# Wider moving operand in the second layer: one matmul of 512 columns in place of two of 256, tiles three to seven

## The chip, the cores and the metric

The kernel runs on one core of a Trainium2 chip. The metric is the device time of one execution in microseconds (us). A core has five engines that run side by side: TensorE (PE, matmuls; its weight loads are listed apart as PEld), VectorE (DVE), ScalarE (ACT), GpSimd (POOL) and SyncE (SP), which here issues the transfers (DMA).

## What is computed

Linear attention with positive random features (8 batches, 8 heads, 576 positions, 64 values per head, 128 features), followed by a layer norm and a two-layer perceptron with a residual. Cut to what matters:

```python
q_p, k_p = phi(q_s), phi(k_s)            # exp(projection - its maximum), 128 features
kv = np.einsum('bhsm,bhsd->bhmd', k_p, v)
z = np.sum(k_p, axis=2)
num = np.einsum('bhsm,bhmd->bhsd', q_p, kv)
den = np.einsum('bhsm,bhm->bhs', q_p, z)[..., None] + 1e-06
x = (num / den)                          # heads side by side: 4608 rows of 512
xn = (x - mu) / np.sqrt(var + 1e-06) * g_ln
ch = np.maximum(xn @ w_ch1, 0.0) @ w_ch2 # 512 -> 2048 -> 512
return x + ch
```

All of it is in 32-bit floats. The product that the change touches is the second one of the perceptron, hidden values (2048) by `w_ch2`.

## The kernel before, in words

**Tiling.** The 4608 rows are nine tiles of 512 rows (`NT`, `T`), each four chunks of 128 rows (`TC`). The 2048 hidden values are 16 blocks of 128 (`NF`). Weights and activations are each split into a rounded high part and a low rest, and a product is three matmuls: high by high, high by low, low by high.

**Three ways through the perceptron.** Tiles 0 and 1 (t < `SEVEN` = 2): the first layer is `mm1`, lines 1335 to 1355, and its matmuls go through the helper `rounded` (line 1299), 512 columns each. Tiles 2 to 6: the first layer is `seven` (line 1385), which computes two by two blocks with seven products instead of eight, each product six matmuls of 256 columns through `product` (line 1380). Tiles 7 and 8 (t >= `DEEP` = 7): both layers work that way, the second one in `deep` and `deep_product` (line 1659).

**The second layer, `mm2` (line 1606).** It serves tiles 0 to 6. One call handles one hidden block f of one tile t: for each of the four row chunks i it adds a 128x128 block of hidden values (stationary, `hl`) times a 128x512 block of weights (moving, `w`) to the bank `accs[i]` of PSUM, in three passes. In tiles 0 and 1 a pass is one matmul of 512 columns through `rounded`. In tiles 2 to 6 it is two matmuls of 256 columns at line 1627, one for each half of the output columns, each with its own weight load. So a call is 12 matmuls of 512 columns in the first two tiles and 24 of 256 columns in the next five. Columns are stored in an interleaved order, so each form reads its moving operand and writes PSUM in short strided pieces; both cover the same 512 output columns.

**The order of the work.** A planner (`Plan`) writes the order of all engines when the kernel is built: each generator says which engine it wants next and for how long, and the planner picks by rank and by its estimate of when each engine is free. `mm2` asks for `us(PE, 3 * 0.2268)` per row chunk (line 1619) whatever the tile. `gen_mlp` (line 1771) strings the perceptron together at the lowest rank: in tiles 2 to 6 `seven` runs four products, then lets one `mm2` call in (`between`), runs three more products, and another `mm2` call follows. Work of higher rank is put between: keys (`joined`, line 797; sums at line 747), queries (`gen_q2`, two matmuls of 512 columns through `rounded`, `om_hi` and `om_lo`) and the numerators of the attention (line 1104). Lines 747, 838, 885 and 1104 are small matmuls that use part of the array.

The evictions of a finished chunk (`result`, line 1638, on DVE) and the stores of the output come after the last block f of a tile.

Of the kernel before, what the change touches and what calls it, by code (L numbers as in the profile page):

```python
# [29 lines left out]
NF = DFF // P  # L30
# [38 lines left out]
class Plan:  # L69
# [74 lines left out]
    def free(self, *names):  # L144
        for n in names:
            assert n not in self.places, n
            self.places[n] = self.cur.seen()
            self.cur.holds -= n[0] == "b" and 0 < self.cur.holds
            self.wake(lambda w: w[0] == "get" and n in w[1])
# [48 lines left out]
def favor_ffn(ctx, tc, kT, kTr, kD, kDr, vF, vR, qT, qD, omT, gT, w1, w2, out):  # L198
# [12 lines left out]
    nc = tc.nc  # L211
# [24 lines left out]
    def us(eng, t):  # L236
        return "run", {eng: t}
# [16 lines left out]
    def wait(*key):  # L254
        return "wait", key
# [13 lines left out]
    def bank(tag, n=512):  # L269
        return tile_of(tag, [P, 512], F32, ps)[:, 0:n]  # L270
# [1026 lines left out]
    def rounded(out, lhsT, rhs, start, stop):  # L1297

        nc.tensor.matmul(  # L1299
            out.rearrange("p (c a b) -> p c a b", a=AW, b=BW), lhsT,  # L1300
            rhs.rearrange("p (a c b) -> p c a b", a=AW, b=BW), start=start, stop=stop,
        )
# [301 lines left out]
    accs = {}  # L1604

    def mm2(t, f):
        yield wait("w", 2, f)
        yield wait("hid", t, f)
        lent = f in LENT
        if lent and t >= SEVEN:  # L1610
            yield wait("back", t, f)
        t_h, hl = hid[t, f]
        w = wparts[2, f]
        for i in range(TC):
            if f == 0:
                t_b = yield "get", (b_acc[i],)
                accs[i] = bank(t_b)
            cs = slice(i * P, (i + 1) * P)
            yield us(PE, 3 * 0.2268)
            if t < SEVEN:  # L1620
                rounded(accs[i], hl[:, 0, cs], w[:, 0], start=(f == 0), stop=False)
                rounded(accs[i], hl[:, 0, cs], w[:, 1], start=False, stop=False)
                rounded(accs[i], hl[:, 1, cs], w[:, 0], start=False, stop=(f == NF - 1))
            else:
                for l, r in ((0, 0), (0, 1), (1, 0)):
                    for n in range(2):
                        nc.tensor.matmul(  # L1627
                            accs[i].rearrange("p (c a b) -> p c a b", a=AW, b=BW)[:, :, n * 8 : n * 8 + 8], hl[:, l, cs],
                            w[:, r, n * HC : (n + 1) * HC].rearrange("p (a c b) -> p c a b", b=BW, c=4),
                            start=f + l + r + n == 0, stop=f == NF - 1 and l == 1, skip_group_check=True,  # L1630
                        )
            if f == NF - 1:
                plan.add(URGENT + 50, result(t, i, accs[i]))
        free(t_h)
        if lent and t >= SEVEN - 1:
            free(*n_w[2, f + HOSTS if t >= SEVEN and f in SHARED else f])

    def result(t, i, acc):
        c = t * TC + i
        t_x, x = xs[c]  # L1640
        yield wait("rs", t)
        yield dve(DM)
        nc.vector.scalar_tensor_tensor(
            out=x, in0=acc, scalar=rss[:, c : c + 1], in1=x, op0=ALU.mult, op1=ALU.add
        )
        free(b_acc[i])
        yield dma(P * DM)
        nc.sync.dma_start(out[c * P : (c + 1) * P], x)
        free(t_x)
# [121 lines left out]
    def gen_mlp():  # L1771
# [8 lines left out]
        for t in range(NT):  # L1780
            for f in range(NF if t < SEVEN else NF // 2):
                if f == 0 and t < SEVEN:
                    yield from one()
                if t < SEVEN:
                    if t == f == 0:
                        yield from opening(OPEN)
                    elif t or f >= OPEN:
                        yield from mm1(t, f)
                    yield from one()
                    last.append(mm2(t, f))  # L1790
                else:
                    g, h = divmod(f, 2)
                    yield from seven(t, g, h, one)
                    yield from one()
                    if t < DEEP:
                        last += [mm2(t, NK * g + h), mm2(t, NK * g + 2 + h)]
                    else:
                        last += [deep(t, f, FRONTS), deep(t, f, BACKS)]
            if t >= DEEP:
                last.append(deep_late(t))  # L1800
# [47 lines left out]
AW, BW = 16, 8  # L1848
# [9 lines left out]
SEVEN, HC = 2, DM // 2  # L1858
# [72 lines left out]
```

## Time and profile before

| | |
|---|---|
| time, median of 3 runs | 926.13 us (925.30 to 926.68) |
| the profiled execution's own time | 925.38 us |
| its span, first to last instruction | 923.3 us |
| TensorE busy | 915.2 us (99%), 8893 matmuls and as many weight loads |
| VectorE busy | 794.7 us (86%) |
| ScalarE busy | 520.3 us (56%) |
| GpSimd busy | 139.0 us (15%) |
| line 1627, the matmuls in question | 1920, 239.1 us busy |
| granted TensorE clock, mean | 0.999 |

The profile's times are those of one execution. Matmuls are pipelined: a matmul starts while the one before is still in the array, so the duration that is listed for one is longer than the distance between two starts, and the busy time of a group is the union of its matmuls' spans. The timeline merges consecutive instructions of a kind into one row: its start, the time from its first start to its last end, and the count behind the x.

### The profile page before, as it was taken

Reading aid. Unit: us, or ns where it says so; the run is one execution under the profiler, and the core shown is the slowest. Engines: PE = TensorE matmul, PEld = TensorE weight load, DVE = VectorE, ACT = ScalarE, POOL = GpSimd, SP = SyncE. Lnnn points to the kernel's source line nnn. Section 1 sums busy time; section 2 is a strip of 40 time slices with the busy share of each in tenths; the row PEclk is TensorE's granted clock in tenths of the full one; section 3 lists DMA queues with packets and bytes.
Section 4 is the critical chain, followed back from the end, with each engine's and each line's share of the span. In section 5 each row is a group of like instructions: output and inputs, shape, how many; then the busy total and the mean of one; then the engine's idle time right before and its main releaser. Section 6 shows DMA issues by size and latency. Waiting matters only on the chain.

```text
span 923.3 us, 23130 instructions
## 1 busy us (share of the span) xinstructions
PE 915.2 (99%) x8893; PEld 855.1 (93%) x8893; DVE 794.7 (86%) x1810; ACT 520.3 (56%) x1227; POOL 139.0 (15%) x80
## 2 busy tenths in 40 slices
PE   9999999999999999999999999999999999999998
PEld 7787788888889999999999999999999999999997
DVE  7999998978987899879988899889888889778766
ACT  6687755545556467645754576456654544453442
POOL 3301423200221012201111032011201310000000
PEclk9999999999999999999999999999999999999999
DMA  9179852368897998898898998898777869999981
GB/s 346 71 260 381 276 179 94 92 184 239 262 306 263 333 332 282 282 346 272 284 322 269 314 336 281 283 343 292 269 233 239 271 195 301 379 327 298 362 285 46
DMA packets 150317, 247.62 MB, mean 268 GB/s; under 512 B 13120, under 2 KB 64448, under 8 KB 150208
## 3 DMA queue, kind: packets, MB, share of 16 engines
q1 hardware_dynamic: 150208, 246.16, 79.4%
q8 instruction: 70, 1.15, 0.5%
q14 instruction: 39, 0.32, 0.1%
HBM read 204.16 MB, written 41.94 MB: 267 GB/s over the span
## 4 chain that ended last, share of the span: by engine, by line
PE 95%; DVE 3%; DMA 1%; issue 0%; POOL 0%; ACT 0%; DVEq 0%; SPq 0%; ACTq 0%
PE b L1380 29%; PE b L1627 24%; PE b L1299 20%; PE b L1659 8%; PE b L747 4%; PE b L1104 4%; PE b L797 2%; PE b L838 2%; PE b L330 1%; PE b L885 1%; PE b L1326 1%; DMA wide<-qD 1%; DVE v L1703 0%; PE b L1284 0%; DVE kp L1748 0%; DVE x L1041 0%
## 5 line engine op out<-in xcount | busy, mean ns | idle before, releaser
L1627 PE MATMUL b<-w,hid 128*128 128x256 f32 x1920 | 239.1, 276 | 0.0
L1627 PEld LDWEIGHTS b<-w,hid 128*128 128x128 f32 x1920 | 229.0, 188 | 2.8
L950 POOL PARTITION_ALL_REDUCE wide<-wide x72 | 137.9, 1938 | 606.1 <-ACT wide L244 328.3
L1380 PE MATMUL b<-xnT,w 128*128 128x256 f32 x1344 | 174.5, 276 | 0.0
L1380 PEld LDWEIGHTS b<-xnT,w 128*128 128x128 f32 x1344 | 162.7, 188 | 1.6
L1380 PE MATMUL b<-w,w 128*128 128x256 f32 x1008 | 126.7, 276 | 0.2 <-DVE hid L1471 0.2
L1443 DVE TENSOR_TENSOR w<-b,w 128x256 f32<-128x256 f32 x224 | 108.5, 484 | 15.7 <-PE b L1380 9.9
L1380 PEld LDWEIGHTS b<-w,w 128*128 128x128 f32 x1008 | 120.2, 188 | 1.5 <-DVE hid L1471 0.4
L1299 PE MATMUL b<-w,hid 128*128 128x512 f32 x384 | 97.2, 392 | 0.0
L1299 PE MATMUL b<-xnT,w 128*128 128x512 f32 x360 | 89.8, 392 | 0.0
L1299 PEld LDWEIGHTS b<-w,hid 128*128 128x128 f32 x384 | 70.7, 188 | 14.9 <-issue 0.3
L1299 PEld LDWEIGHTS b<-xnT,w 128*128 128x128 f32 x360 | 66.5, 188 | 14.6 <-issue 1.0
L812 ACT ACTIVATE kp<-kp,mb 128x128 f32<-128x128 f32 x176 | 64.9, 398 | 18.9 <-DVE mb L809 18.8
L1469 ACT ACTIVATE hid<-w 128x256 fp32r<-128x256 f32 x82 | 42.7, 522 | 49.0 <-PE b L1627 27.8
L244 ACT COPY wide<-b 128x512 f32<-128x512 f32 x70 | 39.9, 584 | 38.8 <-PE b L1299 20.1
L958 ACT ACTIVATE wide<-wide 128x512 f32<-128x512 f32 x72 | 45.5, 633 | 26.9 <-DVE wide L953 26.6
L1471 DVE SCALAR_TENSOR_TENSOR hid<-w,hid 128x256 fp32r<-128x256 f32 x82 | 49.6, 606 | 12.5 <-ACT hid L1469 11.9
L953 DVE TENSOR_TENSOR wide<-wide,wide 128x512 f32<-128x512 f32 x64 | 49.3, 772 | 3.7 <-POOL wide L950 3.5
L1659 PE MATMUL b<-w,wide 128*128 128x256 f32 x348 | 45.3, 275 | 0.0
L914 DVE TENSOR_TENSOR wide<-wide,wide 64x512 fp32r<-64x512 f32 x56 | 41.6, 749 | 2.2 <-ACT wide L912 0.6
L1659 PEld LDWEIGHTS b<-w,wide 128*128 128x128 f32 x348 | 42.1, 188 | 0.0
L1469 ACT ACTIVATE hid<-b 128x256 fp32r<-128x256 f32 x40 | 15.3, 382 | 46.6 <-PE b L1380 41.9
(162 smaller groups left out, 1449.7 us busy)
## 6 DMA issues: line engine op xcount, KB each, us to landing
w<-side SPq DMA_DIRECT2D x224, 256.0 KB, 4.9
w<-kept SPq DMA_DIRECT2D x80, 512.0 KB, 4.7
w<-kept SPq DMA_DIRECT2D x67, 256.0 KB, 5.3
w<-w SPq DMA_DIRECT2D x32, 512.0 KB, 6.3
wide<-qD SPq DMA_DIRECT2D x56, 256.0 KB, 5.2
w<-deep SPq DMA_DIRECT2D x47, 256.0 KB, 5.4
wide<-kD SPq DMA_DIRECT2D x40, 256.0 KB, 5.2
kept<-w SPq DMA_DIRECT2D x16, 512.0 KB, 3.0
```

Source lines behind the costliest of these rows:

```text
L812: nc.scalar.activation(out=kp[:, j], in_=kp[:, j], func=AF.Exp, scale=1.0, bias=mb[:, j : j + 1])
L914: nc.vector.tensor_tensor(out=qs[D:P], in0=qraw[D:P], in1=f32(qs[D:P]), op=ALU.subtract)
L950: nc.gpsimd.partition_all_reduce(mx, qc, P, bass_isa.ReduceOp.max)
L953: nc.vector.tensor_tensor(out=qc, in0=pq if direct else qc, in1=mx, op=ALU.subtract)
L958: nc.scalar.activation(out=qc, in_=qc, func=AF.Exp)
L1299: nc.tensor.matmul(out.rearrange("p (c a b) -> p c a b", a=AW, b=BW), lhsT, rhs.rearrange("p (a c b) -> p c a b", a=AW, b=BW), start=start ...
L1380: nc.tensor.matmul(passes(out), left(k, l), passes(right[:, r, k]), start=start and k + l + r == 0, stop=k + r == 2, skip_group_check=True,)
L1443: nc.vector.tensor_tensor(out=out, in0=left, in1=right, op=ALU.add)
L1469: nc.scalar.activation(out=hl[:, 0, cols], in_=x, func=AF.Relu)
L1471: nc.vector.scalar_tensor_tensor(out=hl[:, 1, cols], in0=x, scalar=0.0, in1=f32(hl[:, 0, cols]), op0=ALU.max, op1=ALU.subtract)
L1627: nc.tensor.matmul(accs[i].rearrange("p (c a b) -> p c a b", a=AW, b=BW)[:, :, n * 8 : n * 8 + 8], hl[:, l, cs], w[:, r, n * HC : (n + 1) ...
L1659: nc.tensor.matmul(out.rearrange("p (c a b) -> p c a b", a=8, b=8), left[:, l, chunk * P : (chunk + 1) * P], right[:, r].rearrange("p (a c ...
```

## The change

The branch on t is removed from `mm2`: the three passes of tiles 2 to 6 go through `rounded`, 512 columns each, as in tiles 0 and 1. Nothing else is edited; the time that the planner is told stays as it was.

```diff
             cs = slice(i * P, (i + 1) * P)
             yield us(PE, 3 * 0.2268)
-            if t < SEVEN:
-                rounded(accs[i], hl[:, 0, cs], w[:, 0], start=(f == 0), stop=False)
-                rounded(accs[i], hl[:, 0, cs], w[:, 1], start=False, stop=False)
-                rounded(accs[i], hl[:, 1, cs], w[:, 0], start=False, stop=(f == NF - 1))
-            else:
-                for l, r in ((0, 0), (0, 1), (1, 0)):
-                    for n in range(2):
-                        nc.tensor.matmul(
-                            accs[i].rearrange("p (c a b) -> p c a b", a=AW, b=BW)[:, :, n * 8 : n * 8 + 8], hl[:, l, cs],
-                            w[:, r, n * HC : (n + 1) * HC].rearrange("p (a c b) -> p c a b", b=BW, c=4),
-                            start=f + l + r + n == 0, stop=f == NF - 1 and l == 1, skip_group_check=True,
-                        )
+            rounded(accs[i], hl[:, 0, cs], w[:, 0], start=(f == 0), stop=False)
+            rounded(accs[i], hl[:, 0, cs], w[:, 1], start=False, stop=False)
+            rounded(accs[i], hl[:, 1, cs], w[:, 0], start=False, stop=(f == NF - 1))
             if f == NF - 1:
                 plan.add(URGENT + 50, result(t, i, accs[i]))
```

## Rows read from the trace of the kernel before

**Rows 1.** The page: busy time of the engines, and the chain that ended last.
```profile
PE 915.2 (99%) x8893; PEld 855.1 (93%) x8893; DVE 794.7 (86%) x1810; ACT 520.3 (56%) x1227; POOL 139.0 (15%) x80
...
PE b L1380 29%; PE b L1627 24%; PE b L1299 20%; PE b L1659 8%; PE b L747 4%; PE b L1104 4%; PE b L797 2%; PE b L838 2%; PE b L330 1%; PE b L885 1%; PE b L1326 1%; DMA wide<-qD 1%; DVE v L1703 0%; PE b L1284 0%; DVE kp L1748 0%; DVE x L1041 0%
```

**Rows 2.** Windows: window and length, busy time (count) of each engine, clock, DMA.
```profile
275.90:770.50 494.60, 494.60 (x5292) 485.39 (x5291) 432.51 (x1008) 288.16 (x686) 79.24 (x43) 1.00 0.86 287
```

**Rows 3.** Groups by line and shape: busy us, mean ns, idle before.
```profile
L1627 PE MATMUL b<-w,hid 128*128 128x256 f32 x1920 | 239.1, 276 | 0.0
...
L1299 PE MATMUL b<-w,hid 128*128 128x512 f32 x384 | 97.2, 392 | 0.0
```

**Rows 4.** Timeline of PE, third tile: start us, length us, what.
```profile
275.99 2.88 PE L1627 MATMUL b<-w,hid 128*128 128x256 f32 x24
278.71 0.84 PE L1380 MATMUL b<-xnT,w 128*128 128x256 f32 x6
```

**Rows 5.** Timeline of PE, second tile, at 172 us.
```profile
172.52 2.80 PE L1299 MATMUL b<-w,hid 128*128 128x512 f32 x12
175.16 1.49 PE L1299 MATMUL b<-xnT,w 128*128 128x512 f32 x6
```

**Rows 6.** Timeline of PE at 247 us, four rows of x12 between these starts.
```profile
247.29 2.92 PE L1299 MATMUL b<-w,hid 128*128 128x512 f32 x12
...
258.35 1.54 PE L1299 MATMUL b<-w,hid 128*128 128x512 f32 x6
```

**Rows 7.** The chain that ended last, at 213 us: start, length, what.
```profile
212.82 1.43 PE b L1104 x44
214.25 20.26 PE b L1299 x87
```

**Rows 8.** Timeline of PE at 234 us, line 797 around line 1299.
```profile
234.35 0.63 PE L797 MATMUL b<-om_both,wide 128*128 128x256 f32 x4
234.82 2.92 PE L1299 MATMUL b<-w,hid 128*128 128x512 f32 x12
237.58 0.65 PE L797 MATMUL b<-om_both,wide 128*128 128x256 f32 x4
238.06 2.94 PE L1299 MATMUL b<-xnT,w 128*128 128x512 f32 x12
```

**Rows 9.** Timeline of PE at 434 us, two query pairs in a row.
```profile
434.18 0.39 PE L1299 MATMUL b<-wide,om_hi 128*128 128x512 f32 x1
...
435.09 0.84 PE L1627 MATMUL b<-w,hid 128*128 128x256 f32 x6
```

**Rows 10.** Timeline of PE at 262 us, products behind a run of line 1299.
```profile
262.04 2.22 PE L1380 MATMUL b<-w,w 128*128 128x256 f32 x18
264.09 0.84 PE L1380 MATMUL b<-xnT,w 128*128 128x256 f32 x6
```

**Rows 11.** Timeline of PE, line 1627 behind lines 747 and 1104.
```profile
302.12 1.66 PE L1627 MATMUL b<-w,hid 128*128 128x256 f32 x12
303.61 0.84 PE L1380 MATMUL b<-xnT,w 128*128 128x256 f32 x6
...
697.18 2.33 PE L1627 MATMUL b<-w,hid 128*128 128x256 f32 x18
```

**Rows 12.** Timeline of PE at 105 us, line 1299 behind line 747.
```profile
103.10 2.09 PE L747 MATMUL b<-v,kp 128*64 128x65 f32 x64
105.11 2.91 PE L1299 MATMUL b<-w,hid 128*128 128x512 f32 x12
107.96 1.14 PE L885 MATMUL b<-wide,om 64*128 64x256 f32 x8
```

**Rows 13.** Timeline of PE at 621 us, line 1627.
```profile
620.87 1.54 PE L1627 MATMUL b<-w,hid 128*128 128x256 f32 x12
622.25 0.39 PE L1299 MATMUL b<-wide,om_hi 128*128 128x512 f32 x1
```

**Rows 14.** Windows, line 1380 on PE alone: length, busy (count), clock, DMA.
```profile
275.90:770.50 494.60, 208.65 (x1659) 1.00 0.86 287
```

## The prediction

> **What bounds the kernel now.** I read the page first. TensorE (PE) is busy for 915.2 of 923.3 us, the chain of work that ended last is 95% PE, and line 1627, which the change removes, is 24% of that chain [rows 1]. Then the windows view of the stretch in which line 1627 runs: from 275.9 to 770.5 us PE is busy for all of the 494.60 us, at a granted clock of 1.00, so at its 2.4 GHz level [rows 2]. In this stretch a nanosecond per matmul is a nanosecond of the end, in either direction. DVE, ACT and the DMA queues only have to keep pace with a PE that never waited for them. The planner charges a group 3 x 0.2268 us on both branches, so it should write the same order on every engine and queue; no step is moved past another and no wait is added.
>
> What a matmul costs can't be read from its mean in the view by line: 276 ns for 256 columns and 392 ns for 512 [rows 3] are durations of overlapping instructions (2 x 276 against 392 would promise 154 us from 960 pairs). Busy time by count is nearer: 239.1/1920 = 125 ns and 97.2/384 = 253 ns, so no gain from the wider form, but these spans hold pipeline tails. What counts is the distance from start to start, and the timeline gives it.
>
> **The change, step by step.** 1920 matmuls of 256 columns with 1920 weight loads become 960 of 512 with 960 loads. 24 of the old ones (12 of the new ones) make up the product of one hidden block, so there are 1920/24 = 80 groups.
>
> *Old price.* In the third tile a group starts at 275.99 and the next matmul at 278.71 [rows 4]: 2.72 us for 24, 113.3 ns each, 226.6 ns for the pair that one new matmul replaces.
>
> *New price.* The trace has the new instruction already: line 1299 does the second layer of the first two tiles, from the same tiles, as 128x512 [rows 3]. It comes at two paces. From 172.52 to 175.16 us twelve of them take 2.64 us, 220.0 ns each [rows 5]. From 247.29 to 258.35 us four dozen, of both layers, take 11.06 us, 230.4 ns each [rows 6]. Both are at full clock. At 2.4 GHz 512 columns alone are 213.3 ns and 256 are 106.7 ns: the old form pays 6.7 ns over its columns, the new one 6.7 ns at its quick pace and 17.1 ns at its slow one. So everything hangs on which pace the new groups get.
>
> I take the slow one, for this reason. Two things lead into a run of 512s. Behind a block of small matmuls that use part of the array (lines 747, 838, 885, 1104) either pace can begin: in the chain of waits 87 of line 1299 behind line 1104 take 20.26 us, 232.9 ns each, start-up included [rows 7]; those of [rows 5] had such a block before them too. But where 512 columns follow directly on 256, the slow pace sets in: twelve of them right behind the four 256-column matmuls of line 797 start at 234.82 and end at 237.58, 2.76 us [rows 8]. From the third tile on the stream is made of 256-column matmuls, and the 512s that it has, the query pairs of line 1299, fit that second case: four in a row from 434.18 to 435.09 take 0.91 us, 227.5 ns each, not 220 [rows 9]. A new group will sit exactly there, between products of line 1380 and 12 long.
>
> Term 1: 80 groups x (2.76 - 2.72) = **+3.2 us**. Bounds: all at the quick pace, 80 x (2.64 - 2.72) = -6.4 us; all at the settled slow pace, 80 x (12 x 0.2304 - 2.72) = +3.6 us. The value lies near the upper end because the neighbours of its row are those of the new groups.
>
> Term 2: the 256-column matmuls behind a new group. Fours of line 797 before and behind slow 512s take 0.47 and 0.48 us [rows 8] instead of 4 x 113.3 = 0.45; but the 18 of line 1380 behind another slow run take 2.05 us [rows 10], 0.01 over 18 x 113.3 = 2.04. Most new groups are followed by a block of line 1380, so I take the 0.01: 80 x 0.01 = **+0.8 us**, with bounds 0 and 80 x 0.03 = 2.4.
>
> Term 3: groups that begin behind a block of small matmuls. The timeline shows 11 such runs of line 1627, the first at 302.12, the last at 697.18 [rows 11]. Twelve 256s take 1.49 us there, 0.13 of it start-up, so 24 would take 2.85; twelve 512s behind such a block took 2.85 from 105.11 to 107.96, and this holds the change to the next small block as well [rows 12], for which I estimate up to 0.1. So between 0 and -0.1 us each, in the middle **-0.5 us** for 11.
>
> Edits at nothing: the weight loads saved, which lie beside the matmuls and leave PE no idle time here [rows 2]; were that cover gone, only fewer loads could help. The evictions and the start flag of a bank keep their places.
>
> Sum: 3.2 + 0.8 - 0.5 = **+3.5 us**. The profiled execution took 925.38 us, so 928.9; the median of the runs is 0.75 us above it, so on that scale 926.13 + 3.5 = **929.6 us**, 0.4% slower.
>
> Here the Trainium skill speaks against me. The quick pace [rows 5] has the same 6.7 ns over its columns as the old form [rows 4], a fixed cost per matmul. The Trainium skill, "TensorE: Matmul & The Clock Gate", section "Back-to-back issue gap", gives the columns over 2.4 GHz plus 2.5 ns at full clock. By it one 512 would save 2.5 ns against two 256s, an estimate of 960 x 2.5 = 2.4 us saved, and the sum would be -2.4 us. The trace agrees with the form of that rule at the quick pace only, and with its 2.5 ns nowhere.
>
> **The rivals.**
> *Faster: one fixed cost instead of two.* If the new groups run at the quick pace, -6.4 us, 919.7. For it: the twelve of [rows 5] are the second layer with its own operands, and the pace, once there, holds for many matmuls. Against it: 512s entered from 256s [rows 8, 9] don't get it. It decides at the first few matmuls of a group: 219 to 221 ns or 226 and up. It is the mechanism of the skill's rule above, with a larger fixed cost.
>
> *Much slower: the disturbed pace doesn't settle.* Behind one small block the 256s themselves are slow, 12 in 1.38 us from 620.87 [rows 13], 115.0 ns instead of 113.3. If after each new group the products stayed at that pace, the 1659 of line 1380 in the stretch [rows 14] would cost 1659 x 1.7 = 2.8 us more: 926.13 + 3.5 + 2.8 = 932.4. Against it: the 18 of [rows 10].
>
> *No change.* The groups keep the pace of their first four, 227.5 ns against 226.6: 960 x 0.9 ns = 0.9 us, 927.0. Groups cut into threes and sixes by query pairs and lines 797 and 747 speak for it, the whole run of 12 in [rows 8] against.
>
> *It doesn't do what it says* (a 512 split in two again): 384 records of 128x512 at line 1299 [rows 3] rule that out.
>
> **How the numbers follow.** Forecast (about +2 to +5 us) 0.61, much slower 0.14, no change 0.10, quick pace 0.15. 0.2% of the time, 1.9 us, is about what a measurement of this kernel can tell from no change. Nearly all of the first two cases lies above it: slower 0.74; within it 0.11; faster 0.15. The range leaves out the quick pace and takes in the others: from 925.8 (no change, with runs 1.2 us lower) to 932.4.
>
> **What would show it.** In the changed profile line 1299 should have 960 more matmuls of 128x512 and line 1627 none. In the timeline a whole group behind line 1380 should take 2.75 to 2.77 us; 2.64 would prove the quick pace and the forecast wrong. The 18 or 24 products behind it should take 0.01 to 0.03 us over 113.3 ns each. PE should stay without idle time in the stretch, and the stretch itself grow from 494.6 to about 498 us. A wait of PE of more than 1 us there, or a changed order, would mean that the sum left something out.

## The result, and the profile after

The changed kernel takes 931.17 us (median of 4, 930.96 to 931.59) against 925.71 us before (median of 4): ratio 1.006, 95% interval 1.0047 to 1.0072. It is 5.5 us slower. The forecast was 3.5, in a case of about +2 to +5; the difference lies a little above that case, the time inside the range of 925.8 to 932.4. The profiled execution took 931.3 us, its span 929.3 us. One of the six runs of the kernel that reads and writes in order, further down, took 4951.69 us where the others took 928.66 to 930.49: its ratio leaves that run out, its median of 929.78 counts it.

The page of the changed kernel, busy time of the engines and the chain that ended last:

```profile
PE 921.1 (99%) x7933; PEld 817.6 (88%) x7933; DVE 795.7 (86%) x1810; ACT 521.1 (56%) x1227; POOL 138.1 (15%) x80
...
PE b L1299 44%; PE b L1380 29%; PE b L1650 8%; PE b L747 4%; PE b L1104 4%; PE b L797 2%; PE b L838 2%; PE b L330 1%; PE b L885 1%; PE b L1326 1%; DMA w<-side 0%; DVE v L1694 0%; DVE wide L914 0%; PE b L1284 0%; DVE kp L1739 0%; DVE x L1041 0%
```

960 matmuls and 960 weight loads are gone; PE is still what bounds, and its busy time went up by 921.1 - 915.2 = 5.9 us [rows 1], as much as the span (6.0). Where PE spends it, from the groups by line and shape of the changed kernel (busy us, mean ns, idle before):

```profile
L1299 PE MATMUL b<-w,hid 128*128 128x512 f32 x1344 | 339.2, 392 | 0.0
L1380 PE MATMUL b<-xnT,w 128*128 128x256 f32 x1344 | 175.2, 277 | 0.0
L1380 PE MATMUL b<-w,w 128*128 128x256 f32 x1008 | 127.6, 277 | 0.3 <-DVE hid L1471 0.3
...
L797 PE MATMUL b<-om_both,wide 128*128 128x256 f32 x176 | 27.5, 278 | 0.0
...
L330 PE MATMUL b<-spin 128*128 128x256 bf16 x117 | 19.0, 301 | 1.2 <-DVE spin L292 1.2
```

The same view of the kernel before, the groups that [rows 3] leave out:

```profile
L1380 PE MATMUL b<-xnT,w 128*128 128x256 f32 x1344 | 174.5, 276 | 0.0
L1380 PE MATMUL b<-w,w 128*128 128x256 f32 x1008 | 126.7, 276 | 0.2 <-DVE hid L1471 0.2
...
L797 PE MATMUL b<-om_both,wide 128*128 128x256 f32 x176 | 27.1, 275 | 0.0
...
L330 PE MATMUL b<-spin 128*128 128x256 bf16 x117 | 18.2, 292 | 1.2 <-DVE spin L292 1.2
```

The second layer, lines 1299 and 1627 together, took 97.2 + 239.1 = 336.3 us [rows 3] and takes 339.2 now: +2.9 us. Line 1380 was not edited and takes 175.2 + 127.6 = 302.8 us; in the kernel before the same two groups stood at 174.5 and 126.7, so +1.6. Line 797 was at 27.1: +0.4. The query pairs of line 1299 took 0.2 more. The rest is nearly all line 330, the filler matmuls at the start: 18.2 before, 19.0 here. That is not put down to the change: in the experiments below it lies between 18.0 and 19.1, whatever was edited. Without it the two profiled executions would differ by 5.1 us instead of 5.9; the medians differ by 5.5.

The timeline of PE, first groups of the third tile (start us, length us, what), answers to [rows 4]:

```profile
276.87 2.92 PE L1299 MATMUL b<-w,hid 128*128 128x512 f32 x12
279.62 0.88 PE L1380 MATMUL b<-xnT,w 128*128 128x256 f32 x6
280.34 0.62 PE L797 MATMUL b<-om_both,wide 128*128 128x256 f32 x4
280.81 1.52 PE L1380 MATMUL b<-xnT,w 128*128 128x256 f32 x12
282.17 2.92 PE L1299 MATMUL b<-w,hid 128*128 128x512 f32 x12
```

In the kernel before, behind the two rows of [rows 4]:

```profile
279.39 0.61 PE L797 MATMUL b<-om_both,wide 128*128 128x256 f32 x4
279.84 1.52 PE L1380 MATMUL b<-xnT,w 128*128 128x256 f32 x12
```

A group takes 279.62 - 276.87 = 2.75 us where it took 2.72. Then comes what I had put too low: the six products behind it take 0.72 us instead of 6 x 113.3 = 0.68, the four of line 797 take 0.47 instead of 0.45, and only the next twelve are back at 1.36. This group costs 0.03 us itself and 0.06 us behind it. Not every group leaves that much: 0.06 for all 80 would be 4.8 us, and lines 1380 and 797 together lost 2.0, which is 0.025 for each. About half of the groups are cut by other work into pieces of three, six or nine matmuls.

The windows view of the stretch (window, length, then busy time and count of PE, PEld, DVE, ACT and POOL, clock, DMA) answers to [rows 2]:

```profile
276.70:776.20 499.50, 499.50 (x4332) 447.55 (x4332) 433.16 (x1007) 288.66 (x686) 78.36 (x43) 1.00 0.85 285
```

PE has no idle time here and the granted clock is 1.00, as before. The stretch is 499.5 us long, 4.9 more. Only the weight loads got idle time, 485.39 us busy before and 447.55 now. And the quick pace exists in the new groups too, but it is rare; the timeline of PE at 379 us shows one such place:

```profile
377.06 2.23 PE L1299 MATMUL b<-w,hid 128*128 128x512 f32 x9
379.13 0.64 PE L797 MATMUL b<-om_both,wide 128*128 128x256 f32 x4
379.61 0.83 PE L1299 MATMUL b<-w,hid 128*128 128x512 f32 x3
380.27 2.20 PE L1380 MATMUL b<-xnT,w 128*128 128x256 f32 x18
382.31 0.61 PE L797 MATMUL b<-om_both,wide 128*128 128x256 f32 x4
```

Nine take 2.07 us, 230 ns each; three of the same group, behind four other matmuls, take 0.66, about 220 ns each. The eighteen products behind these three take 2.04 us, nothing over 18 x 113.3. By the starts in the trace four pieces of three go at this pace, all of them behind line 797; no uncut group does.

### The profile page after: what moved, and what is told of

Its sections match the earlier page's. It is cut to its first block, busy times and chain, and to the rows that moved or that the text cites. A ratio compares the mean times of both kernels' runs of the same rounds, so it can differ in the third digit from the quotient of the medians.

```text
span 929.3 us, 21210 instructions
## 1 busy us (share of the span) xinstructions
PE 921.1 (99%) x7933; PEld 817.6 (88%) x7933; DVE 795.7 (86%) x1810; ACT 521.1 (56%) x1227; POOL 138.1 (15%) x80
## 4 chain that ended last, share of the span: by engine, by line
PE 95%; DVE 3%; DMA 0%; issue 0%; ACT 0%; SPq 0%; DVEq 0%; ACTq 0%
PE b L1299 44%; PE b L1380 29%; PE b L1650 8%; PE b L747 4%; PE b L1104 4%; PE b L797 2%; PE b L838 2%; PE b L330 1%; PE b L885 1%; PE b L1326 1%; DMA w<-side 0%; DVE v L1694 0%; DVE wide L914 0%; PE b L1284 0%; DVE kp L1739 0%; DVE x L1041 0%
## 5 line engine op out<-in xcount | busy, mean ns | idle before, releaser
L1299 PE MATMUL b<-w,hid 128*128 128x512 f32 x1344 | 339.2, 392 | 0.0
L1299 PEld LDWEIGHTS b<-w,hid 128*128 128x128 f32 x1344 | 243.8, 188 | 47.9 <-issue 0.3
L1380 PE MATMUL b<-xnT,w 128*128 128x256 f32 x1344 | 175.2, 277 | 0.0
L1380 PEld LDWEIGHTS b<-xnT,w 128*128 128x128 f32 x1344 | 165.7, 188 | 4.1
L1380 PE MATMUL b<-w,w 128*128 128x256 f32 x1008 | 127.6, 277 | 0.3 <-DVE hid L1471 0.3
L1380 PEld LDWEIGHTS b<-w,w 128*128 128x128 f32 x1008 | 123.4, 188 | 4.2 <-DVE hid L1471 0.5
L1299 PEld LDWEIGHTS b<-xnT,w 128*128 128x128 f32 x360 | 66.5, 188 | 14.6 <-issue 1.0
L244 ACT COPY wide<-b 128x512 f32<-128x512 f32 x70 | 40.0, 585 | 41.3 <-PE b L1299 18.2
L1361 ACT ACTIVATE hid<-b 128x512 fp32r<-128x512 f32 x32 | 19.2, 602 | 38.8 <-PE b L1299 38.6
L1104 PEld LDWEIGHTS b<-kv,wide 128*64 128x64 f32 x1024 | 31.8, 137 | 6.5 <-issue 4.3
```

The lines of the kernel that those rows point to most:

```text
L1104: nc.tensor.matmul(pn[a:z, i + h - h0], phi(c // 2, h, slice(cols + a, cols + z)), kvs[b][1][:, h], start=True, stop=True,)
L1299: nc.tensor.matmul(out.rearrange("p (c a b) -> p c a b", a=AW, b=BW), lhsT, rhs.rearrange("p (a c b) -> p c a b", a=AW, b=BW), start=start ...
L1380: nc.tensor.matmul(passes(out), left(k, l), passes(right[:, r, k]), start=start and k + l + r == 0, stop=k + r == 2, skip_group_check=True,)
```

## The experiments

In all of them only the second layer of tiles three to seven is edited, unless said otherwise. What a group takes is read from the timeline of PE, from its first start to the next start behind it.

**Is it the width?** The forecast blamed the 512 that follows on 256s. Then 256s should keep their pace, whatever the order in which they read. The moving operand lies in SBUF as 16 x 4 pieces of 8 values; a half of 256 columns took eight pieces, four times over (8x4), a 512 takes sixteen, four times over (16x4). Here a half takes sixteen, twice over (16x2):

```diff
-accs[i].rearrange("p (c a b) -> p c a b", a=AW, b=BW)[:, :, n * 8 : n * 8 + 8], hl[:, l, cs],
-w[:, r, n * HC : (n + 1) * HC].rearrange("p (a c b) -> p c a b", b=BW, c=4),
+accs[i].rearrange("p (c a b) -> p c a b", a=AW, b=BW)[:, 2 * n : 2 * n + 2], hl[:, l, cs],
+w[:, r].rearrange("p (a c b) -> p c a b", b=BW, c=4)[:, 2 * n : 2 * n + 2],
```

> Tiles three to seven as before, in pairs of 256 columns, but the pair is cut the other way: each half sweeps the moving operand in sixteen pieces of 8 values two times over (16x2), as one of 512 does four times, instead of eight pieces four times over (8x4). Theory 'width' (a 512 is slow because it is one matmul of 512 behind matmuls of 256): the pace stays 113.3 ns, 24 of a group take 2.72 us, time 925.7 us within 1 us. Rival 'walk' (the sweep of sixteen pieces sets the pace, at any width): 115 ns or more in the group, 2.76 us or more for 24, time 929 us or more.

Measured: 938.15 us, ratio 1.013 (1.0115 to 1.0145). The timeline of PE:

```profile
276.65 3.01 PE L1627 MATMUL b<-w,hid 128*128 128x256 f32 x24
279.50 0.85 PE L1380 MATMUL b<-xnT,w 128*128 128x256 f32 x6
```

24 take 2.85 us, 119 ns each. With the same width and count as before it is slower than the change itself. Theory "width" falls: the walk through the moving operand has a price of its own.

This run also takes the change apart. Its two halves together read the same columns in the same order as one 512 of the changed kernel. So the new order at the old width takes a group from 2.72 to 2.85 us (ratio 1.013), and the greater width in the new order takes it back to 2.75 (ratio 1.006). The first of these steps changes the order of writing too, to which two pairs of kernels further down give no price.

**Two other walks at 512 columns.** Read in the order of SBUF, with the interleaving undone on the writing side (the three calls of `rounded` are written as one line):

```diff
-rounded(accs[i], hl[:, l, cs], w[:, r], ...)
+nc.tensor.matmul(
+    accs[i].rearrange("p (c a b) -> p a c b", a=AW, b=BW), hl[:, l, cs],
+    w[:, r].rearrange("p (a c b) -> p a c b", a=AW, b=BW), ...
```

> The changed kernel, but in tiles three to seven the 512 columns are read in the order in which they lie in SBUF and written to PSUM in scattered pieces of 8. Theory 'width': 230 ns each and a group of 12 in 2.75 to 2.77 us as in the changed kernel, time 931 us within 1 us. Rival 'walk': another pace; 220 ns, a group in 2.64 us and 923 us or less if the scattered read was what slowed it, 240 ns and more, 940 us or more, if reading in order is the worse of the two.

Measured: 928.55 us, ratio 1.003 (1.0019 to 1.0041). The timeline of PE:

```profile
281.09 2.90 PE L1626 MATMUL b<-w,hid 128*128 128x512 f32 x12
283.83 0.84 PE L1380 MATMUL b<-w,w 128*128 128x256 f32 x6
284.51 0.61 PE L797 MATMUL b<-om_both,wide 128*128 128x256 f32 x4
```

A group takes 2.74 us, hardly less than the 2.75 of the changed kernel, but the products behind it take 0.68, their old pace. So 512 columns as such don't leave the after-effect. In the view by shape the groups of this kernel take 241.7 us (242.0 in the changed one) and line 1380 takes 301.5 (302.8): most of what is won lies behind the groups. The time is below what "width" allowed, and neither of the two numbers of "walk" came up.

Swept in eight pieces, eight times over, on both sides:

```diff
+accs[i].rearrange("p (a c b) -> p c a b", a=8, b=8), hl[:, l, cs],
+w[:, r].rearrange("p (a c b) -> p c a b", a=8, b=8), ...
```

> The changed kernel, but in tiles three to seven the 512 columns are swept in eight pieces of 8 values, eight times over (8x8), on the reading and on the writing side alike; the output columns of these tiles so stay in the stored order and the result is not the reference's. Theory 'width': 230 ns each, a group of 12 in 2.75 to 2.77 us, time 931 us within 1 us. Rival 'walk': the quick pace of 220 ns, a group of 12 in 2.64 us, time 919 to 921 us.

Measured: 948.40 us, ratio 1.0241 (1.0226 to 1.0257). The timeline of PE:

```profile
276.87 3.15 PE L1626 MATMUL b<-w,hid 128*128 128x512 f32 x12
279.85 0.86 PE L1380 MATMUL b<-xnT,w 128*128 128x256 f32 x6
```

2.98 us for twelve, 248 ns each. My guess that eight pieces are what makes a quick walk was wrong by 27 us and more in the time. That the walk matters stands firmer for it; which walk is good can't be told from the number of its pieces. The pieces also lie twice as far apart here, every 64 values instead of every 32, and the order of writing changed with that of reading, so this run doesn't say which of these costs the time.

**Is a 512 always a loss?** The kernel before, with line 1299 cut into halves too (both layers of the first two tiles, and the query pairs):

```diff
-nc.tensor.matmul(
-    out.rearrange("p (c a b) -> p c a b", a=AW, b=BW), lhsT, ...
+for n in range(2):
+    nc.tensor.matmul(
+        out.rearrange("p (c a b) -> p c a b", a=AW, b=BW)[:, :, n * 8 : n * 8 + 8], lhsT,
+        rhs[:, n * HC : (n + 1) * HC].rearrange("p (a c b) -> p c a b", b=BW, c=4), ...
```

> The kernel before with every matmul of 512 columns at line 1299 cut into two of 256 as well (both layers of tiles one and two, and the query pairs). Theory 'two paces' (512s are as often at 220 ns as at 230 in the first two tiles, so their mean of some 226.5 ns is that of two 256s): time 925.7 us within 1 us. Rival 'a 512 always loses' (744 of them at 230.6 against 226.6): 3 us gained, 922.7 us.

Measured: 927.04 us, ratio 1.0009 (0.9999 to 1.0019). Groups by line and shape of this kernel:

```profile
L1300 PE MATMUL b<-w,hid 128*128 128x256 f32 x768 | 97.7, 278 | 0.0
L1300 PE MATMUL b<-xnT,w 128*128 128x256 f32 x720 | 90.4, 278 | 0.0
```

97.2 us became 97.7 for the second layer [rows 3]; nothing is gained, and the rival that a 512 always loses is out. In the first two tiles, with their mixture of the two paces, one 512 costs what two 256s cost.

**Reading side or writing side?** The 512s read in order, written in order as well; against the kernel read in order this changes the writing order alone:

```diff
-accs[i].rearrange("p (c a b) -> p a c b", a=AW, b=BW), hl[:, l, cs],
+accs[i], hl[:, l, cs],
```

> 512 columns in tiles three to seven, read in order and written in order too, so that the output columns of these tiles stay in the stored order and the result is not the reference's. It differs from the changed kernel in the reading order alone, and from the kernel read in order and written in scattered pieces in the writing order alone. Theory 'reading walk': as that kernel, 227 ns behind the first two matmuls of a group, 2.74 us for a group of 12, 928.5 us within 1 us. Rival 'writing walk' (what the scattered pieces in PSUM cost): 220 ns, 2.64 us, 919 to 922 us. Theory 'width': 931 us.

Measured: 929.78 us, ratio 1.0033 (1.002 to 1.0047). The timeline of PE:

```profile
276.87 2.90 PE L1626 MATMUL b<-w,hid 128*128 128x512 f32 x12
279.61 0.84 PE L1380 MATMUL b<-xnT,w 128*128 128x256 f32 x6
```

2.74 us again, and 241.7 us for all the groups in both kernels: the order in which PSUM is written costs nothing here. From the changed kernel this one differs in the reading order alone. The description of `mm2` ahead of the prediction has both forms write PSUM in short pieces, but the destination of `rounded` is cut as (c a b) and walked as c, a, b, so a 512 of the changed kernel is written in one run; only the halves of the kernel before are written in pieces, four runs of 64. The difference to the changed kernel is small: 929.78 us against 931.17, ratios 1.0033 and 1.006 with intervals that touch.

**The same walk at half the width.** Halves read in order, first written in scattered pieces, then written in order:

```diff
-accs[i].rearrange("p (c a b) -> p c a b", a=AW, b=BW)[:, :, n * 8 : n * 8 + 8], hl[:, l, cs],
-w[:, r, n * HC : (n + 1) * HC].rearrange("p (a c b) -> p c a b", b=BW, c=4),
+accs[i].rearrange("p (c a b) -> p a c b", a=AW, b=BW)[:, n * 8 : n * 8 + 8], hl[:, l, cs],
+w[:, r, n * HC : (n + 1) * HC].rearrange("p (a c b) -> p a c b", b=BW, c=4),
```

> Tiles three to seven in pairs of 256 columns as in the kernel before, but each half is read in order and written to PSUM in scattered pieces of 8: the same walk as in the 512s that were read in order, at half the width. Theory 'walk, not width': 113.3 ns, a group of 24 in 2.72 to 2.74 us, 925.9 to 928.5 us. Rival 'width': clearly under the 512s of that walk, which took 928.5 us, so 925.9 us or less. Rival 'reading in order is bad at 256': 115 ns or more, 930 us or more.

Measured: 939.61 us, ratio 1.0143 (1.0128 to 1.0158). The timeline of PE:

```profile
276.30 3.04 PE L1627 MATMUL b<-w,hid 128*128 128x256 f32 x24
279.18 0.86 PE L1380 MATMUL b<-xnT,w 128*128 128x256 f32 x6
```

```diff
+accs[i][:, n * HC : (n + 1) * HC], hl[:, l, cs],
+w[:, r, n * HC : (n + 1) * HC],
```

> Pairs of 256 columns in tiles three to seven, read in order and written in order; the output columns of these tiles stay in the stored order and the result is not the reference's. Theory 'walk, not width': the pace is the one of the 512s read and written in order, per column. If a matmul pays a fixed cost of its own on top of its columns, the pair costs more than one such 512 by 6.7 ns, 6.4 us over 960 pairs; if all is per column, the two kernels agree within 1 us apart from what the first matmuls of a group cost.

Measured: 939.36 us, ratio 1.0143 (1.0128 to 1.0158). The timeline of PE, second group of the third tile:

```profile
281.39 3.04 PE L1627 MATMUL b<-w,hid 128*128 128x256 f32 x24
284.27 0.86 PE L1380 MATMUL b<-w,w 128*128 128x256 f32 x6
```

Both take 2.88 us for 24, 120 ns each, and again the writing order is free. The 512s of this walk took 2.74 for the same work: here the wide form gains 0.14 us per group, 11 us over 80 (the times differ by 11.1 and 9.6), where the fixed cost per matmul that I had named would give 6.4. So "walk, not width" is wrong as well: it is the two together, and the rival "reading in order is bad at 256" came true. Halves are good in the one walk that the kernel before uses and bad in two others. In both orders that were run at both widths the 512 is the cheaper form: 2.75 against 2.85 us in sixteen pieces, 2.74 against 2.88 in order.

**Does the weight load disturb the reading?** While a matmul streams its moving operand, the next weight load reads SBUF too [rows 2, the PEld column]. If the two readers collide, another walk of the load should shift the pace. Three kernels, the change, the kernel before and the halves read in order, take every fourth column instead of 128 neighbours:

```diff
-cs = slice(i * P, (i + 1) * P)
+cs = slice(i * P, (i + 1) * P) if t < SEVEN else slice(i, T, TC)
```

> The changed kernel, but in tiles three to seven the weight loads take every fourth column of the 512 hidden rows instead of 128 neighbouring ones; the rows of these tiles land in other places of the output, which is not the reference's. Work and counts are the same. Theory 'two readers' (the moving operand and the next weight load read SBUF at the same time and disturb each other): the sequence 227, 226, 226, 234, 234, 239 of a group changes by more than 2 ns per matmul, the group by more than 0.03 us, the time by more than 2 us either way. Rival 'moving walk alone': the same sequence, 2.757 us for a group, 931.2 us within 1 us.

> The kernel before with the same strided weight loads in tiles three to seven, output rows in other places, not the reference's. Theory 'two readers': 24 of a group leave 2.72 us by 0.03 us or more (upwards, since 113.3 ns is the quickest pace seen), 928 us or more. Rival 'moving walk alone': 113.3 ns, 925.9 us within 1 us.

> The pairs of 256 columns read in order (120 ns each, 939.6 us) with the same strided weight loads, output rows in other places, not the reference's. Theory 'two readers': the 120 ns change by more than 1 ns, the time by more than 2 us, most likely downwards to 113 to 118 ns and 926 to 936 us. Rival 'moving walk alone': 120 ns, 939.4 us within 1 us.

Measured: 947.79 us (ratio 1.0233, 1.0204 to 1.0263), 1157.41 us (1.2497, 1.246 to 1.2533) and 1156.39 us (1.2486, 1.2449 to 1.2522). The timeline of PE of the first:

```profile
275.93 3.13 PE L1299 MATMUL b<-w,hid 128*128 128x512 f32 x12
278.89 0.84 PE L1380 MATMUL b<-xnT,w 128*128 128x256 f32 x6
279.57 0.61 PE L797 MATMUL b<-om_both,wide 128*128 128x256 f32 x4
```

its group once more, without the first matmul:

```profile
276.28 2.77 PE L1299 MATMUL b<-w,hid 128*128 128x512 f32 x11
```

of the second:

```profile
277.43 5.78 PE L1627 MATMUL b<-w,hid 128*128 128x256 f32 x24
283.05 0.85 PE L1380 MATMUL b<-xnT,w 128*128 128x256 f32 x6
```

and of the third:

```profile
276.78 5.77 PE L1627 MATMUL b<-w,hid 128*128 128x256 f32 x24
282.38 0.87 PE L1380 MATMUL b<-xnT,w 128*128 128x256 f32 x6
```

The groups by line, weight loads (busy us, mean ns), of the kernel before and of the second:

```profile
L1627 PEld LDWEIGHTS b<-w,hid 128*128 128x128 f32 x1920 | 229.0, 188 | 2.8
...
L1627 PEld LDWEIGHTS b<-w,hid 128*128 128x128 f32 x1920 | 459.5, 329 | 1.7
```

All times moved by more than 2 us, as theory "two readers" had it, but far more than either theory said, the third not downwards as guessed, and for another reason: the load itself became slow. 24 halves take 5.62 us, 234 ns each (5.60 in the third kernel, with the other walk), and a load is listed with 329 ns instead of 188. Both walks now have the same pace, so the halves seem to wait for loads. A 512 needs half as many. Its group of twelve takes 2.96 us, of which the first matmul takes 276.28 - 275.93 = 0.35 and the other eleven 237 ns each, so the load seems to be the limit here too. The test doesn't answer its question. It does show one thing more: the six products behind this slow group take 0.68 us, so a slow group doesn't always leave an after-effect. The Trainium skill, "TensorE: Matmul & The Clock Gate", section "Step-by-step: what each phase is for", says that the two reads use ports of their own and that loading takes no bandwidth from the running matmul. No run here shows whether that holds for loads of neighbouring columns.

## Why the prediction was right, point by point

**The bound** was read rightly: PE was full before and is full now, its extra busy time is the extra span, no wait appeared. The wait of line 1380 went from 0.2 to 0.3 us.

**Terms 1 and 3, the groups**, +3.2 and -0.5 us. Measured: +2.9 us busy for both, where 2.7 were forecast. The twelve 512s behind line 797 [rows 8] were the right row to take: 2.76 there, 2.75 in the new groups. The quick pace, which the rival needed, came up only in four pieces of three. Term 3 was mis-sized: the eleven runs behind small blocks, each from its first start to the next start behind it, took 20.63 us before and take 20.58 now, so it is -0.05 and term 1 about +2.9. That the two misses nearly cancel is luck. The first of the eleven, 1.49 us before [rows 11] and 1.42 now, is one of the two that gained more than 0.01:

```profile
303.34 1.59 PE L1299 MATMUL b<-w,hid 128*128 128x512 f32 x6
304.76 0.86 PE L1380 MATMUL b<-xnT,w 128*128 128x256 f32 x6
```

**Term 2, the matmuls behind a group**, +0.8 us, was mis-sized by more than any other, and is the step that fell short. It measured 1.6 us on line 1380 and 0.4 on line 797, 2.0 together, near the upper bound of 2.4. I had two rows, the 0.48 us for four [rows 8] and the 0.01 us over eighteen [rows 10], and took the second because blocks of line 1380 follow most groups. But that row stands behind a run of more than sixty 512s [rows 6, 10], and the state that a run leaves isn't the same after twelve: 0.72 us for six and 0.47 for four. The row to take was the one behind exactly twelve: 80 x 0.03 = 2.4. Why a longer run leaves less behind is not shown. The 0.2 us of the query pairs had no term.

**The rival "much slower"** had its place right and its size wrong: the disturbed pace does carry into line 1380, but it fades within some ten matmuls. The 931.17 us lie between the forecast of 929.6 and this rival's 932.4.

**The reason behind term 1** was only half of it. I said that a 512 entered from 256s is slow. The runs show that 256s are slow too in two walks of three (119 and 120 ns) and that 512s with another walk and the same neighbours take 2.74 us for twelve and leave nothing behind. What the change did is two things at once: it replaced the order of the 8x4 halves, the best of those tried at 256, by that of sixteen pieces, which costs 0.13 us per group, and it made the matmul wider, which gives 0.10 back. The query pairs [rows 9] were also misread as the slow pace: 77 of the 82 query matmuls in the stretch go at 226 or 227 ns, which is what two 256s cost and the pace of the rival "no change". A new group begins like that, 227, 226 and 226 ns, and slows from its fourth matmul on. The forecast held because the rows of term 1 had the very walk and neighbours of the new groups, not because its reason was complete.

**The rule that spoke against it** is that of the Trainium skill, "TensorE: Matmul & The Clock Gate", section "Back-to-back issue gap", which gives it there for a matmul by itself. Its saving of 2.5 ns for each matmul less was not seen: the trace has +3 ns per 512 in the changed kernel. Between kernels that read in the same order fewer matmuls do save time, but more: 8 ns per 512 in sixteen pieces (2.75 against 2.85 us per twelve) and 12 ns in order (2.74 against 2.88).

**Still open:** why a walk through the moving operand slows PE by 1 to 10%, and what decides between 220 and 230 ns for the same instruction. Whether the reading of the next weights has a part in it was tried and not settled. No version tried beats the kernel before; the best with 512s is the one read in order, 0.3% behind.

## What to carry to other kernels

Where PE is the bound, price a matmul by the distance from start to start in a stretch with the same reading pattern and the same neighbours, and price the matmuls behind it too: here two thirds as much was lost on lines that were not edited as on the one that was. At the same reading order the wider matmul was the cheaper one in both comparisons here. The change lost because it altered that order along with the width, so look at what else an edit of the width does to the order in which the moving operand is read, and measure the two apart. The order in which PSUM is written was free in both pairs that differed in nothing else.

## What the runs showed of the hardware that was not expected

- At a granted clock of 1.00, 256 columns of 32-bit values take 113, 119 or 120 ns, depending on the order in which they are read (8x4, 16x2, in order), and 512 columns 229, 228 or 248 ns (16x4, in order, 8x8 with the pieces twice as far apart; mean over a group of twelve).
- A weight load that takes every fourth 32-bit column instead of neighbouring ones took a matmul of 256 columns from 113 to 234 ns, 231 us on 1920 of them; the same stride cost 960 matmuls of 512 columns some 17 us against the changed kernel.
- In the changed kernel a whole group leaves the next ten matmuls or so slower than usual (0.72 us instead of 0.68 for six, 0.47 instead of 0.45 for four), on other operands and in another bank. The 512s read in order (2.74 us) and the ones with strided weight loads (2.96 us) leave none: 0.68 for six.
